# Moving three query loads and one pair of row copies to later steps in a fused attention and feed-forward kernel

## The chip, the cores and the metric

The kernel runs on one core of one Trainium2 chip, in one launch. The metric is the device time of that launch in microseconds (us); lower is better. Five engines work side by side, each through its own list of instructions in order: TensorE (PE in the profile; its weight loads are PEld), VectorE (DVE), ScalarE (ACT), GpSimd (POOL) and SyncE (SP). They meet at semaphores. POOL and SP also issue the transfers (DMAs) between the chip's main memory and its on-chip memory.

## The reference, cut to what matters

Inputs `q`, `k`, `v` have 4 batches, 8 heads, 768 positions and 64 numbers a head. Attention runs in chunks of 32 queries; each chunk sees 8 memory rows, 16 positions to the left and 8 to the right of itself. Its output is the input of a feed-forward block with a normalisation ahead of it and a residual.

```python
for c in range(nc):                       # chunks of 32
    q_c = q[:, :, c_start:c_end]
    k_full = concatenate([mem_k, k[:, :, l_start:r_end]])
    v_full = concatenate([mem_v, v[:, :, l_start:r_end]])
    scores = scale * matmul(q_c, k_full.T)
    a = softmax(scores)
    out[:, :, c_start:c_end] = matmul(a, v_full)
...
x = out.transpose(0, 2, 1, 3).reshape(B, S, H * D)          # 4 x 768 x 512
mu, var = mean(x), mean((x - mu) ** 2)
xn = (x - mu) / sqrt(var + 1e-06) * g_ln
return x + maximum(xn @ w_ch1, 0.0) @ w_ch2                 # 512 -> 2048 -> 512
```

## The kernel before

**Tiles and units.** The 4 x 768 tokens are 24 tiles of 128 (`t`), six to a batch; two tiles make a unit `u`, of 256 tokens, and there are 12 units. For a tile, `qk` makes scores on TensorE (`qk_products`, line 322), takes off the maximum on VectorE and exponentiates on ScalarE; `pt` transposes the weights P (line 353) and copies them on ScalarE (line 361); `val` multiplies them with V (line 373), normalises on VectorE (`tokens`) and subtracts the mean (`shift`, line 396, on POOL here); `root` squares on ScalarE (line 409) and makes the inverse root on POOL (lines 416 and 420); `turn_x` transposes the result (line 429) and copies it. A unit then goes up to 2048 in eight products (`up`, line 464) and down to 512 in seven (`down7`, line 643), the latter one unit behind.

**How the order is made.** Nothing is scheduled by a planner: the order on each engine is that in which the program is written. Up to unit 2 and from unit 8 on it is written out by hand. Units 3 to 7 are a loop over 16 steps: an even step ends with `up(u, step // 2)`, an odd one with `down7(u - 1, step // 2)`, and whatever `at(u, step, fn, ...)` put into the plan runs ahead of it, in the order in which it was put there.

**The loads of batches 2 and 3.** They are spread over the plan:

- `load_octets(i, half, src, b, lo, n)`, line 104, issues two DMAs on POOL (one for even, one for odd heads; each 48 partitions of 4 x 512 numbers, 192 KB in 16 bit, converted from 32 bit on the way) into `raw[i][half]`; `i` is 0 for k and 1 for q.
- `mix(i, half, engine)` copies `raw` into another order (line 261), k on VectorE at step 12 of the same unit and q on ScalarE at step 5 of the next. `later_k` and `later_q` transpose that on TensorE (line 274) and copy it into the key and query tiles.
- `load_v_head`, `load_v_ends`: V's rows, straight to their places, in runs of 128 bytes, also issued on POOL (lines 116, 121, 127, 131).
- `v_mem(b)`, line 155: two DMAs issued on SP (line 158), 120 KB each, which copy the memory rows from `memv16` (8 partitions) to two places of every group of V. `v_shared` (line 153), also on SP, copies rows of V that two groups share.

Batch 2's second half of k and q is loaded in unit 3, batch 3's halves in units 5 and 6. The first tile of batch 2, number 12, reaches `val` at step 4 of unit 5; the first of batch 3, number 18, right behind the loop.

**Stores.** SP also issues the stores of finished tiles (`store`, line 656, 256 KB), at the sixth and seventh part of `down7`, that is at steps 11 and 13.

**Waits that a program adds.** A DMA of POOL or SP waits for the DMA that last used its completion semaphore; POOL's take eight in turn, so each waits for the one eight DMAs back. Whatever stands behind a waiting instruction on its engine waits too.

Of the kernel before, what the change touches and what calls it, by code (L numbers as in the profile page):

```python
# [18 lines left out]
def kernel(  # L19
# [1078 lines left out]
    def at(u, step, fn, *args):  # L1098
        plan.setdefault((u, step), []).append((fn, args))
# [16 lines left out]
    for b in range(2, B):  # L1116
        u0 = 3 * b - 3
        for half in range(2):
            w = u0 - 1 + half
            if w > 2:  # L1120
                at(w, 1, load_octets, 0, half, k, b, 48 * half, 48)
                at(w, 3, load_octets, 1, half, q, b, 48 * half, 48)
                at(w, 12, mix, 0, half, "V")
            at(w + 1, 5, mix, 1, half, "A")
            for n, step in enumerate((1, 7 if w == 2 else 6, 11, 15)):
                if n < 2:
                    at(w + 1, step, later_k, b, half, n, "V")
                else:
                    at(w + 1, step, later_q, b, half, n - 2, "A")
            for n in range(8):  # L1130
                if w > 2:
                    step = (0, 2, 4, 12, 13, 14, 15, 16)[n]
                    at(w, step, load_v_head, b, 4 * half + n // 2, n % 2)
                else:
                    at(4, n // 2, load_v_head, b, n // 2, n % 2)
        at(u0 + 1, 0, load_v_ends, b)
        at(u0 + 1, 10 if b == 2 else 6, v_shared, b, 0, NG)
        if b == 2:
            at(3, 8, v_mem, b)
        else:  # L1140
            at(u0 + 1, 6, v_mem, b)
        at(u0, 14, mem_cols, KT[b % 2], memT[:, 4 * b : 4 * b + 4, :])
        at(u0, 14, mem_ends, KT[b % 2], memT[:, 4 * b : 4 * b + 4, :])
# [332 lines left out]
```

## Time and profile before

| What | Value |
|---|---|
| runs of the kernel, us | 224.4, 223.35, 224.49; median 224.4 |
| the profiled execution, us | 224.4 |
| its span, first to last instruction, us | 222.7 |
| mean granted TensorE clock | 0.997 |
| POOL's DMA queue (q0) | 38,416 packets, 14.48 MB, 56.3% of 16 engines' span |
| SP's DMA queue (q1) | 5,092 packets, 8.02 MB, 12.1% |
| queue of kind "instruction" (q8) | 28 packets, 0.46 MB, 0.8% |
| queue of kind "instruction" (q14) | 10 packets, 0.08 MB, 0.1% |

The profile describes one execution. Its span leaves out what lies ahead of the first and behind the last instruction, here 224.4 - 222.7 = 1.7 us. Times within it count from the span's start. Busy times are per engine and overlap; a share of the DMA queues is the time that their packets took against 16 engines working all the span. In the timeline, a bracket behind a row holds the idle time ahead of it on its engine and what ended it. The five units of the loop begin (first `up` product of each) at 70.28, 88.71, 105.71, 121.44 and 138.43 us; the loop's last product of the kind ends it at 155.40 us.

### The profile page before, as it was taken

The numbers are of one execution on the slowest core, as the hardware profiler recorded it, in microseconds if no ns is written. First come the engines' busy times: TensorE is split into PE (matmuls) and PEld (weight loads), VectorE is DVE, ScalarE is ACT, GpSimd is POOL, SyncE is SP. The second block draws the span as 40 slices with busy tenths as digits, with TensorE's granted clock in tenths as the row PEclk, the third lists the DMA queues.
The fourth block names the chain that finished last, engine by engine and source line by source line (L and its number), as shares of the span: only waits on it lengthen the run. The fifth ranks groups of instructions, "written<-read, shape, count | busy, mean of one in ns | idle before, by whom it ended". The sixth has DMA issues, their size and how long they took to land.

```text
span 222.7 us, 8335 instructions
## 1 busy us (share of the span) xinstructions
PE 212.9 (96%) x3581; PEld 187.3 (84%) x3581; DVE 175.9 (79%) x388; ACT 132.8 (60%) x262; POOL 134.2 (60%) x210
## 2 busy tenths in 40 slices
PE   6987999999999998999999999999999999999992
PEld 2555877789989988999989999999899899999981
DVE  1588767888898995994785996994889986888982
ACT  3198875886785397378347288288667734654000
POOL 7958399989999428947346937414377549830000
PEclk9999999999999999999999999999999999999998
DMA  5999999999998994993933993952000102001223
GB/s 74 193 205 204 213 212 207 136 168 149 119 99 106 185 97 71 141 84 86 180 43 88 133 112 71 103 95 84 25 3 3 39 11 81 17 4 49 94 97 96
DMA packets 43770, 23.24 MB, mean 104 GB/s; under 512 B 30068, under 2 KB 40372, under 8 KB 43684
## 3 DMA queue, kind: packets, MB, share of 16 engines
q0 software_dynamic: 38416, 14.48, 56.3%
q1 hardware_dynamic: 5092, 8.02, 12.1%
q8 instruction: 28, 0.46, 0.8%
q10 hardware_dynamic: 224, 0.20, 0.3%
q14 instruction: 10, 0.08, 0.1%
HBM read 29.02 MB, written 6.29 MB: 159 GB/s over the span
## 4 chain that ended last, share of the span: by engine, by line
PE 86%; DMA 9%; POOL 2%; issue 1%; DVE 0%; POOLq 0%
PE upb L464 22%; PE dnb L643 22%; DMA w1c<-in_moe_w_ch_dram 6%; PE one L464 5%; PE one L643 5%; PE dnb L464 4%; PE upb L643 4%; PE two L373 3%; DMA raw<-in_q_dram 3%; PE one L274 3%; PE dnb L578 2%; PE one L578 2%; PE one L322 2%; POOL raw L107 2%; PE one L353 2%; PE upb L490 2%
## 5 line engine op out<-in xcount | busy, mean ns | idle before, releaser
L464 PEld LDWEIGHTS <-w1c 128*128 128x128 f16 x640 | 67.3, 114 | 1.6 <-DMA w1c<-in_moe_w_ch_dram 0.4
L464 PE MATMUL upb<-xT,w1c 128*128 128x256 f16 x456 | 59.2, 274 | 0.0
L456 ACT ACTIVATE rT<-upb 128x512 f16<-128x512 f32 x55 | 32.1, 597 | 17.0 <-PE upb L464 16.7
L650 DVE SCALAR_TENSOR_TENSOR xs<-dnb,rstd,xs 128x256 f32<-128x256 f32 x55 | 26.3, 478 | 11.6 <-PE dnb L643 10.8
L643 PEld LDWEIGHTS <-RS 128*128 128x128 f16 x320 | 30.3, 98 | 3.2
L344 ACT ACTIVATE P<-sub 128x512 f16<-128x512 f32 x24 | 15.1, 632 | 22.3 <-DVE sub L334 22.3
L416 POOL TENSOR_SCALAR veps<-ssq 128x1 f32<-128x1 f32 x24 | 5.9, 248 | 35.0 <-ACT sq L409 34.1
L643 PEld LDWEIGHTS <-rT 128*128 128x128 f16 x240 | 22.9, 98 | 2.3
L643 PE MATMUL dnb<-T,RS 128*128 128x256 f16 x184 | 23.9, 273 | 0.0
L396 POOL TENSOR_SCALAR xn<-xs,nmean 128x512 f16<-128x512 f32 x17 | 12.6, 740 | 17.7 <-DVE nmean L389 13.5
L637 DVE TENSOR_TENSOR RS<-rT 128x1024 f16<-128x1024 f16 x18 | 13.5, 754 | 5.4 <-ACT rT L456 5.2
L409 ACT ACTIVATE sq<-xs,nmean 128x512 f16<-128x512 f32 x24 | 17.3, 721 | 0.2
L383 DVE CUSTOM_DVE_ANT_1 xs<-two,rec 128x512 f32<-128x512 f32 x24 | 16.6, 691 | 0.8
L643 PE MATMUL dnb<-w2c,rT 128*128 128x256 f16 x120 | 15.4, 273 | 0.0
L420 POOL TENSOR_TENSOR rstd<-veps,mhalf 128x1 f32<-128x1 f32 x24 | 13.8, 573 | 2.0
L116 POOL DMA_DIRECT2D V<-in_v_dram x16 | 13.5, 844 | 0.8 <-PE dnb L643 0.7
L241 DVE COPY KT<-one 128x192 f16<-128x192 f16 (+1 forms) x20 | 10.2, 548 | 3.3 <-PE one L228 2.5
L464 PE MATMUL one<-xT,w1c 128*128 128x256 f16 x96 | 12.5, 273 | 0.2 <-DMA w1c<-in_moe_w_ch_dram 0.2
L274 PEld LDWEIGHTS <-raw 96*128 96x128 f16 x192 | 10.4, 97 | 1.6 <-issue 1.1
L464 PE MATMUL dnb<-xT,w1c 128*128 128x256 f16 x88 | 11.3, 274 | 0.0
L361 ACT COPY PT<-one 128x512 f16<-128x512 f16 x14 | 8.2, 584 | 4.6 <-PE one L353 4.6
L373 PEld LDWEIGHTS <-PT 64*32 64x32 f16 x768 | 7.3, 93 | 4.2 <-issue 3.1
(197 smaller groups left out, 484.1 us busy)
## 6 DMA issues: line engine op xcount, KB each, us to landing
out_dram<-xs SPq DMA_DIRECT2D x21, 256.0 KB
raw<-in_k_dram POOLq DMA_DIRECT2D x16, 192.0 KB, 5.5
raw<-in_q_dram POOLq DMA_DIRECT2D x12, 192.0 KB, 5.5
w1c<-in_moe_w_ch_dram POOLq DMA_DIRECT2D x4, 512.0 KB, 11.8
w2c<-in_moe_w_ch_dram POOLq DMA_DIRECT2D x4, 512.0 KB, 14.0
V<-in_v_dram POOLq DMA_DIRECT2D x16, 77.0 KB, 3.8
raw<-in_v_dram POOLq DMA_DIRECT2D x4, 192.0 KB, 6.8
V<-V SPq DMA_DIRECT2D x2, 360.0 KB
```

The costliest lines, as they stand in the source:

```text
L116: nc.gpsimd.dma_start(out=V[b % 2][72:128, 0 : NG - 1, h, 0:64], in_=dram(v, base + 16 * D, [[64, 56], [64 * 64, NG - 1], [1, 64]]),)
L274: nc.tensor.matmul(out=pv[:, rows * r : rows * r + rows], lhsT=m[0:rows, jj, r, :], rhs=identity[0:rows, 0:rows], is_transpose=True, start ...
L344: nc.scalar.activation(out=P[t % 3], in_=sub[t % 2], func=ACTF.Exp, scale=0.125)
L373: nc.tensor.matmul(out=two[col : col + 32, 128 * h : 128 * h + 65], lhsT=PT[t % 3][rows, 2 * (h // 4) + h % 2, q0 : q0 + 32], rhs=V[b % 2] ...
L383: nc.vector.tensor_tensor_reduce(out=x.rearrange("p (h d) -> p h d", h=H), in0=free(two, 0, [[128, 8], [1, 64]]), in1=free(r, 0, [[1, 8], ...
L409: nc.scalar.activation(out=sq, in_=xs[t % 9], func=ACTF.Square, bias=nmean[t % 6], scale=1.0, accum_out=ssq[i],)
L420: nc.gpsimd.tensor_tensor(out=rstd[t % 9], in0=veps[i], in1=mhalf, op=ALU.pow)
L456: nc.scalar.activation(out=o, in_=i, func=ACTF.Relu)
L464: nc.tensor.matmul(out=p[:, 256 * hb : 256 * hb + 256], lhsT=free(w1c[hc // 4][:, dt, :], hc % 4, [[4, 128]]), rhs=xT[u % 3][:, dt, :], st ...
L637: nc.vector.tensor_tensor(out=R[k][:, lo:hi, :], in0=a[:, lo:hi, :], in1=b[:, lo:hi, :], op=op)
L643: nc.tensor.matmul(out=p[:, 0:256], lhsT=left[:, n, :], rhs=right(n), start=(n == 0 and not add), stop=(n == 7), skip_group_check=add,)
L650: nc.vector.scalar_tensor_tensor(out=x, in0=p[:, 0:256], scalar=rstd[t % 9], in1=x, op0=ALU.mult, op1=ALU.add,)
```

## The change

Two lines of the plan. Within units 3 and 5 the query load moves from step 3 to step 10, within unit 6 from step 3 to step 8. Batch 2's memory rows move from step 8 to step 12 of unit 3, which on SP is from ahead of unit 3's first store (step 11) to behind it.

```diff
             if w > 2:
                 at(w, 1, load_octets, 0, half, k, b, 48 * half, 48)
-                at(w, 3, load_octets, 1, half, q, b, 48 * half, 48)
+                at(w, 10 if w < 6 else 8, load_octets, 1, half, q, b, 48 * half, 48)
                 at(w, 12, mix, 0, half, "V")
...
         if b == 2:
-            at(3, 8, v_mem, b)
+            at(3, 12, v_mem, b)
         else:
             at(u0 + 1, 6, v_mem, b)
```

`w` is the unit in which a half of batch `b` is loaded. On TensorE, VectorE and ScalarE the order of instructions is the same as before. On POOL each of the three pairs of query DMAs now stands behind the shifts of both tiles of its unit, one V load and the first root, and ahead of the second root. No instruction is added or taken away.

## The prediction

> **What bounds the kernel now.** First the page's head: TensorE is busy nearly throughout, so only what leaves TensorE idle, or makes it do more, can set the end.
>
> ```profile
> span 222.7 us, 8335 instructions
> PE 212.9 (96%) x3581; PEld 187.3 (84%) x3581; DVE 175.9 (79%) x388; ACT 132.8 (60%) x262; POOL 134.2 (60%) x210
> ```
>
> Second, busy time by stretches, cut where the timeline shows the first up product of units 3, 4, 5, 6 and 7 (columns: stretch, length, then busy time and count of PE, PEld, DVE, ACT, POOL, granted clock, DMA share, GB/s).
>
> ```profile
> 70.28:88.71 18.43, 17.49 (x307) 16.16 (x306) 15.18 (x36) 11.26 (x21) 9.99 (x18) 1.00 0.92 117
> 88.71:105.71 17.00, 17.00 (x301) 15.81 (x298) 13.30 (x29) 11.17 (x21) 12.25 (x21) 1.00 0.97 103
> 105.71:121.44 15.73, 15.66 (x268) 14.39 (x266) 12.21 (x27) 8.53 (x17) 7.09 (x12) 1.00 0.62 97
> 121.44:138.43 16.99, 16.99 (x298) 15.67 (x297) 14.22 (x34) 10.69 (x20) 11.85 (x21) 1.00 0.94 112
> ```
>
> Only unit 3 has visible idle PE time: 18.43 - 17.49 = 0.94 us. Third, the chain of waits there: it stands inside one group of eight transposes (L274, line 274), after the seventh, and the releaser is "issue", so no data, semaphore or engine was waited for.
>
> ```profile
> 83.13 0.30 PE one L274 x7
> 83.43 0.94 issue
> 84.37 0.22 PE one L274
> ```
>
> A second, shorter hold stands in unit 5, in the middle of the score products (L322): 32 matmuls took 0.67 us there and 0.44 us in unit 6, 0.23 us more.
>
> ```profile
> 113.80 0.67 PE L322 MATMUL one<-KT,QD 64*32 64x64 f16 x32
> 130.21 0.44 PE L322 MATMUL one<-KT,QD 64*32 64x64 f16 x32
> ```
>
> What are the two? Count TensorE's instructions from where the first ends to where the second ends (84.36 to 114.09): 511 matmuls and 512 weight loads, 1,023. That is four times 256 but for one (a record can be missing). The DMA view has a queue of kind "instruction", q8: 28 packets of 16 KB in the run, 16,384 / 256 = 64 bytes an instruction. From 70.2 to 81.9 it moved nothing; its next packet lies in 81.9 to 83.0:
>
> ```profile
> q0 software_dynamic: 2485, 0.91, 89.4%
> q1 hardware_dynamic: 497, 0.77, 27.9%
> ...
> q0 software_dynamic: 240, 0.09, 66.5%
> q8 instruction: 1, 0.02, 5.6%
> ```
>
> (First two lines: 70.2 to 81.9; last two: 81.9 to 83.0.) Likewise none from 100.0 to 111.7, then one in 111.7 to 112.7. The packets begin at 81.97 and 111.72, last 0.98 and 0.94 us, and TensorE goes on 1.42 and 1.43 us after their ends. So I read both as TensorE out of instructions: block fetched late. Counted in TensorE instructions ahead of need, the fetch in quiet stretches starts 276 ahead (199.77 to 214.63) or 238 (98.89 to 109.34); these two started 38 and 110 ahead. At the normal lead the first would have started at about 75.9: it came 6 us late, while POOL's queue alone held 89% of 16 engines. [...]
>
> **The change, part by part.**
>
> *Nothing is added or removed.* TensorE, VectorE and ScalarE keep their instructions in the same order. On POOL three pairs of query loads (L107, 192 KB each) each move behind five instructions (two shifts, a V load, the two of a root); on SP two copies of the mem rows (L158, 120 KB each) move behind one store.
>
> *Taken out of the late fetch's way, unit 3.* Between 70.4 and 72.9 us the queues took: two stores, two k loads, two mem copies, a V load, two q loads. The loads of 1 KB packets landed slowly:
>
> ```profile
> L107 POOL DMA_DIRECT2D raw<-in_q_dram x2: 574/590/606, 72.3 to 72.9; - x2
> DMA to landing us min/median/max: 6.0/9.2/11.5
> ```
>
> Both q loads (384 packets of 1 KB, half of the 768 that ran until 83.8) and both mem copies (192 packets, 76.2 to 81.6) leave this stretch. By the q and k packets' pace in unit 5 (768 in 105.9 to 113.6, 100 per us) 384 fewer free 3.8 us, the mem copies some more; the fetch must start by 81.97 - 1.10 = 80.9, and 3.8 us earlier than 81.97 is 78.2. Gain between 0 (fetch still late) and the whole hold; I take the whole. Its size: unit 3 less unit 6, its twin in work, is 18.43 - 16.99 = 1.44 us; 0.44 of it is two extra transposes of P (L353, 0.22 us each on the chain); 1.00 us remains. Using unit 6 as the floor includes what ScalarE would take back: in unit 6 the transposes of x (L429, at 135.90) start 0.12 us late behind ScalarE's copy of PT, and unit 3 has that copy at 84.51 to 85.09, just where TensorE will then arrive (86.17 - 1.1 = 85.07).
>
> *Unit 5.* q leaves 106.3 to 107.5 us, half of the 1 KB packets; the fetch (started 111.72) was short by 0.23 us and 3.8 us are freed. Gain 0 to 0.23; I take 0.23.
>
> *Where they go, POOL.* Unit 3's pair lands behind the shift of step 8 (ends 83.69), ahead of the root:
>
> ```profile
> 83.01 0.68 POOL L396 TENSOR_SCALAR xn<-xs,nmean 128x512 f16<-128x512 f32 x1
> 84.70 0.19 POOL L416 TENSOR_SCALAR veps<-ssq 128x1 f32<-128x1 f32 x1 [1.01 <-ACT sq L409]
> ...
> 95.39 0.62 POOL L121 DMA_DIRECT2D V<-in_v_dram  x1
> 96.05 0.71 POOL L396 TENSOR_SCALAR xn<-xs,nmean 128x512 f16<-128x512 f32 x1
> ```
>
> Two issues at 0.59 us fill the 1.01 us of idle and push the root, fifteen V loads and the shift at 96.05 by 0.17 us. Who waits: the transposes L429 at 98.89, which arrive about 1.0 earlier, 97.9; the shift would end at 96.05 + 0.71 + 0.17 = 96.9. Cover 1.0 us, so 0. Were POOL made to wait (each load waits on the semaphore of the one eight back), the cover is smaller: the tightest had 1.1 us to spare (issued 86.17, landed 4.4 us later, reused at 91.70). Pushed by all of q's 3.8 us it would wait 2.7 and cost 1.7 us. I take 0, since the DMAs idle at 7% from 83.7 to 85.0 and can take q first, and POOL in unit 6 ran V loads right behind q without a wait. In units 5 and 6 the pairs fall ahead of ScalarE-bound roots, into 2.82 and 1.26 us of idle: 0.
>
> *Landings.* q is read by ScalarE's copies (L261) in the next unit: 96.66 in unit 4, so 95.6 then; issued at 83.7 and 84.3, with unit 5's worst 7.1 us, it lands by 91.4; with the worst row, 11.5, at 95.8, a cost of 0.2. Unit 7's copy runs at 146.38, q is issued near 134: 0. Mem rows: issued near 87 instead of 71.4, first read by L373 at 109.30: 0. SP's next store starts some 0.5 us later; nothing waits for it.
>
> *Next fetch.* In unit 4 one starts at 93.99 (195 instructions ahead), ends 95.05, and is needed at 97.84: spare 97.84 - 95.05 - 1.42 = 1.4 us. q should be through by 89, so 0; else see the second rival.
>
> Sum: 1.00 + 0.23 = 1.23 us. The profiled execution took 224.4 us (span 222.7 and 1.7 around it), equal to the median of the three runs. After unit 7 no idle on TensorE of this kind is seen, so the gain lasts: 224.4 - 1.2 = 223.2 us, 0.55% less.
>
> **The rivals.**
>
> *The load backlog is not what delays the fetch; nothing changes.* For it: one of the three runs took 223.35, 1.05 us less than the median, about one such hold, so the hold may come and go by itself. Against: the lag rises with 1 KB packets in flight at both places. Then 224.4 us. [...]
>
> *The late fetch moves to unit 4; slower.* There q, both mem copies, two stores and the V loads now meet in 84 to 95 us, where the DMA share is already 1.12 to 1.26. The fetch at 93.99 becomes late once it slips by over 1.4 us, and decides for slower once it slips by over 1.4 + 1.2 = 2.6. With unit 3's 6 us lag (it is 1.1 today) it slips 5, costs 3.6 and the time is 224.4 - 1.2 + 3.6 = 226.8. Against: no 1 KB packets are left then by my count, and under V loads alone lags were 1 to 2 us.
>
> *POOL's queue of V loads slips and x's transposes wait in unit 4.* 0.5 to 1.7 us as above: 223.7 to 224.9, say 224.2.
>
> *Only unit 3's hold goes half, or not unit 5's:* 223.6.
>
> **How the numbers follow.** Forecast 0.62, no effect 0.12, unit 4's fetch 0.08, POOL's slip 0.09, partial 0.09. A measurement of this kernel can tell about 0.5% (1.1 us) from no change, so the line lies at 223.3. The forecast, with ±0.4 us of its own, has some four fifths below it or better, and some of the rivals none: faster 0.58; slower 0.10 (unit 4's fetch and the end of POOL's slip); same 0.32. The range goes from 222.6 (forecast, and the small holds of 0.1 us gone as well) to 224.5, which takes in "no effect" and most of POOL's slip; the forecast's own range is 222.7 to 223.6.
>
> **What would show it.** Right: no "issue" on the chain in unit 3, its stretch at about 17.4 us; L322 in unit 5 at 0.44 us; an instruction packet before 80.9. Wrong: an "issue" of any size in unit 4, idle PE before L429 there released by xn, or the 0.94 us still in place while the q packets are gone.

## The result and the profile after

| | median, us | range, us | runs |
|---|---|---|---|
| before | 223.51 | 222.72 to 224.49 | 6 |
| after | 227.12 | 225.25 to 228.35 | 6 |

The changed kernel is slower: ratio 1.0157, 95% interval 1.0122 to 1.0193, where 0.55% less was forecast. Its profiled execution took 225.25 us, the shortest of its six runs; why the others take about 2 us more is taken up with the experiments, and stays open in part.

First the page's head of the changed kernel, and its busy time by stretches, cut again at the first up product of units 3, 4, 5, 6 and 7 (columns as in the prediction).

```profile
span 223.5 us, 8335 instructions
PE 213.2 (95%) x3581; PEld 187.4 (84%) x3581; DVE 175.2 (78%) x388; ACT 132.8 (59%) x262; POOL 134.2 (60%) x210
```

```profile
70.17:87.58 17.41, 17.41 (x307) 16.13 (x305) 15.13 (x36) 11.16 (x21) 9.72 (x17) 1.00 0.67 95
87.58:106.80 19.22, 17.18 (x301) 15.74 (x299) 13.49 (x29) 11.27 (x21) 13.95 (x23) 1.00 1.27 126
106.80:122.29 15.49, 15.49 (x268) 14.35 (x266) 12.21 (x27) 8.43 (x17) 6.56 (x12) 1.00 0.61 96
122.29:139.29 17.00, 17.00 (x298) 15.69 (x297) 14.25 (x34) 10.69 (x20) 11.84 (x20) 1.00 0.88 97
```

Unit 3 went from 18.43 to 17.41 us and unit 5 from 15.73 to 15.49: the 1.02 and 0.24 us that the prediction promised (1.00 and 0.23). But unit 4 went from 17.00 to 19.22. The sum, -1.02 - 0.24 + 2.22 = +0.96, is the difference of the two profiled executions (225.25 - 224.4 = 0.85) but for 0.1 us in the start-up.

TensorE's timeline in unit 4 shows the new hold, ahead of the transposes of x; first the kernel before, then the changed one:

```profile
98.89 0.39 PE L429 MATMUL one<-identity,xn 128*128 128x128 f16 x4
```

```profile
96.86 1.06 PE L464 MATMUL upb<-xT,w1c 128*128 128x256 f16 x8
99.97 0.40 PE L429 MATMUL one<-identity,xn 128*128 128x128 f16 x4 [2.04 <-POOL xn L396]
```

It waits for xn of tile 10, the shift on POOL. POOL's timeline there, again the kernel before (the row at L131) and then the changed one:

```profile
91.18 0.53 POOL L131 DMA_DIRECT2D V<-in_v_dram  x1
```

```profile
85.82 0.70 POOL L121 DMA_DIRECT2D V<-in_v_dram  x1
...
90.84 0.63 POOL L127 DMA_DIRECT2D V<-in_v_dram  x1
94.25 0.53 POOL L131 DMA_DIRECT2D V<-in_v_dram  x1 [2.77 <-DMA V<-in_v_dram]
...
99.22 0.70 POOL L396 TENSOR_SCALAR xn<-xs,nmean 128x512 f16<-128x512 f32 x1
```

POOL stands still for 2.77 us at L131: this load reuses the completion semaphore of the V load issued eight DMAs earlier, at 85.82, and that one has not landed. All that stands behind it on POOL, six V loads and the shift, moves back; the shift runs at 99.22 instead of 96.05. The landing of that V load (us from issue: least, median, most) before and after:

```profile
DMA to landing us min/median/max: 2.8/2.8/2.8
```

```profile
DMA to landing us min/median/max: 8.1/8.1/8.1
```

85.82 + 8.1 = 93.9, and POOL goes on at 94.25. What slowed it is seen in the DMA view of 90 to 92 us (queue; packets, MB, share of 16 engines), first the kernel before, then the changed one:

```profile
q0 software_dynamic: 1967, 0.22, 180.2%
q1 hardware_dynamic: 65, 0.11, 14.5%
```

```profile
q1 hardware_dynamic: 131, 0.20, 84.7%
q0 software_dynamic: 208, 0.02, 36.9%
```

POOL's queue (q0) moved 208 packets in place of 1,967, though eight V loads were waiting in it. SP's queue (q1) held the two mem-row copies (80 packets of 1,280 bytes) and a store (46 of 2,048), and its 131 packets took 0.847 x 16 x 2 / 131 = 0.21 us each. A store alone does not do this: in the kernel before, SP's packets in the same 2 us are a store's, and POOL's queue ran on beside them.

### The profile page after: what moved, and what is told of

Its sections match the earlier page's. It is cut to its first block, busy times and chain, and to the rows that moved or that the text cites. A ratio compares the mean times of both kernels' runs of the same rounds, so it can differ in the third digit from the quotient of the medians.

```text
span 223.5 us, 8335 instructions
## 1 busy us (share of the span) xinstructions
PE 213.2 (95%) x3581; PEld 187.4 (84%) x3581; DVE 175.2 (78%) x388; ACT 132.8 (59%) x262; POOL 134.2 (60%) x210
## 4 chain that ended last, share of the span: by engine, by line
PE 87%; POOL 5%; DMA 4%; DVE 1%; issue 1%; ACT 1%; POOLq 0%
PE upb L464 23%; PE dnb L643 22%; PE one L464 5%; PE one L643 5%; PE dnb L464 4%; PE upb L643 4%; DMA raw<-in_v_dram 4%; PE two L373 3%; PE one L274 3%; POOL raw L107 2%; PE dnb L578 2%; PE one L578 2%; PE one L322 2%; PE one L353 2%; PE upb L490 2%; PE one L429 2%
## 5 line engine op out<-in xcount | busy, mean ns | idle before, releaser
L420 POOL TENSOR_TENSOR rstd<-veps,mhalf 128x1 f32<-128x1 f32 x24 | 14.3, 597 | 2.0
L445 DVE TENSOR_TENSOR xT<-one,g_col 128x512 f16<-128x512 f16 x13 | 8.9, 685 | 3.2 <-PE one L429 3.0
L373 PEld LDWEIGHTS <-PT 64*32 64x32 f16 x768 | 7.4, 93 | 4.3 <-issue 3.1
L334 DVE TENSOR_TENSOR sub<-one,nmx 128x512 f32<-128x512 f32 x15 | 10.4, 691 | 0.6
```

Source lines behind the costliest of these rows:

```text
L373: nc.tensor.matmul(out=two[col : col + 32, 128 * h : 128 * h + 65], lhsT=PT[t % 3][rows, 2 * (h // 4) + h % 2, q0 : q0 + 32], rhs=V[b % 2] ...
L420: nc.gpsimd.tensor_tensor(out=rstd[t % 9], in0=veps[i], in1=mhalf, op=ALU.pow)
```

## The experiments

Theory A: the mem-row copies, meeting the V loads, hold them up; POOL then waits for a semaphore, and the shift behind it on POOL is late for TensorE. Theory B: the query loads, now ahead of the V loads in POOL's own queue, do it alone.

**The query loads alone**, and **the mem rows alone** (edits against the changed kernel).

```diff
-            at(3, 12, v_mem, b)
+            at(3, 8, v_mem, b)
```

> The three query loads stay at their later steps, the two mem-row copies go back to step 8 of unit 3. Theory A (the mem-row copies, issued near 86 us with the two stores, hold up the V loads, and POOL then waits 2.8 us at L131 for the V load eight back): POOL's wait at L131 goes, the V load issued near 85.8 lands within 6 us instead of 8.1, TensorE's wait for xn in unit 4 is under 0.3 us, the instruction stalls stay away, and the time is 222 to 223, against 223.5 before and 227.1 with the change. Theory B (the query loads ahead of the V loads alone do it): POOL waits 2 to 3 us as in the changed kernel, TensorE waits about 2 us for xn, 226 to 227.5.

```diff
-                at(w, 10 if w < 6 else 8, load_octets, 1, half, q, b, 48 * half, 48)
+                at(w, 3, load_octets, 1, half, q, b, 48 * half, 48)
```

> Only the mem-row copies move behind unit 3's first store; the query loads stay at step 3. Theory A: the copies meet the V loads at 88 to 93 us and slow them as in the changed kernel; with no query loads ahead of the V loads the first V load still lands early, so POOL waits for a later one or little: 223.5 to 225.5. Theory B: no wait of POOL, time 223 to 223.7 (the instruction stall in unit 3 shorter by what the copies no longer take).

Query loads alone: 223.34 us, ratio to before 0.9997 (0.9976 to 1.0018): the loss is gone, but the time is that of the kernel before and not the 222 to 223 expected. Between 84 and 105 us POOL waits for no landing and TensorE for no xn. The V load at 85.74 lands in 4.0 us, and the DMA view of 90 to 92 us of that run shows POOL's queue at full pace:

```profile
q0 software_dynamic: 2297, 0.26, 212.3%
```

Theory B falls. Mem rows alone: 224.14 us, ratio 1.0025 (1.0001 to 1.0049), inside the range of theory A. V loads land in 4.9 and 7.1 us, POOL's queue moves 859 packets in 90 to 92, and the waits of 84 to 105 us (who, for whom: us in total, times, longest) are

```profile
POOL V L116 <- DMA V<-in_v_dram: 1.9, 1, 1.9
...
PE one L429 <- POOL xn L396: 0.9, 1, 0.9
```

So the copies suffice to make the wait, and the query loads ahead, harmless alone, make it longer: 2.0 us on TensorE for both together.

**The mem rows later still**, behind the V loads.

```diff
-            at(3, 12, v_mem, b)
+            at(4, 10, v_mem, b)
```

> Query loads late as in the change; the mem-row copies later still, behind the copy of V's shared rows at step 10 of unit 4 (issued near 98 us, when the V loads have landed). Theory A: no POOL wait at L131, no TensorE wait for xn in unit 4, no instruction stall: 222 to 223, as with the query loads alone. Theory B: 226 to 227.5 as with the change.

223.54 us, ratio 1.0002 (0.9979 to 1.0025): the loss is gone, as theory A asks, but the time is that of before, not the 222 to 223 expected. Its profiled execution, the fastest of its twelve runs (222.69 us), has no hold left in units 3 to 7:

```profile
span 221.0 us, 8335 instructions
```

**The wait, taken off TensorE's way.** The change in full, with tile 10's shift on ScalarE.

```diff
-            at(u, step, val, t)
+            at(u, step, val, t, *(("A",) if t == 10 else ()))
```

> The whole change, but tile 10's shift in unit 4, which stands behind the V loads on POOL, is done by ScalarE. Both theories on what slows the V loads: POOL still waits about 2.8 us at L131, but if that wait costs time only through xn of tile 10, TensorE no longer waits for it and the time falls from 227.1 to 222.3 to 223.5. If something else in the change costs the time (its TensorE clock, the root behind the same queue, later loads), it stays at 225 to 227.

223.9 us, ratio 1.001 (0.9987 to 1.0033), a little above the range expected. POOL still waits, and no L429 row is left among the waits of 84 to 160 us; TensorE's one row there is of another kind:

```profile
POOL V L131 <- DMA V<-in_v_dram: 2.4, 1, 2.4
...
PE one L322 <- issue: 0.7, 1, 0.7
```

Of the change's 3.6 us, about 3.2 (227.12 - 223.9, medians of different rounds) go this way: through one shift behind one queue, with whatever follows such a wait. The row at L322 is a late instruction fetch in unit 5 (its packet ended at 112.96, TensorE went on at 114.42), although the query load is moved away from there in this kernel too. Eleven of the twelve runs took 222.93 to 224.88 us, one 227.41.

**The amount of copying.** Once more the same two copies, and one of the two only.

```diff
             at(3, 12, v_mem, b)
+            at(3, 12, v_mem, b)
```

> The changed kernel with the two mem-row copies of unit 3 issued a second time right behind the first (same data to the same places). Theory (the copies hold up the V loads): they run about 4.7 us longer beside the V loads, POOL's wait grows from 2.8 by 1 to 4 us, and the time from 227.1 to 228 to 231. Rival (the order on SP and the semaphores make the wait, not the copies' traffic): 227 as with the change.

```diff
-            at(3, 12, v_mem, b)
+            at(3, 8, v_mem, b, 0, NG, (32,))
+            at(3, 12, v_mem, b, 0, NG, (64,))
```

(`v_mem` takes the list of its places here.)

> The whole change, but only one of the two mem-row copies stands behind the store; the other is back at step 8. Theory (the copies' traffic holds up the V loads, by its amount): the V load issued near 85.7 lands between 4.0 us (no copy there) and 8.1 us (both) after issue, POOL's wait is 0 to 1.5 us in place of 2.8, TensorE's wait for xn in unit 4 under 1.2 us, and the time 223.3 to 224.8. Rival (one copy is enough, as any SP transfer there delays POOL): the wait stays over 2.3 us and the time is 226 to 227.5.

| copies beside the V loads | first V load's landing, us | POOL's waits for landings, us | TensorE's wait for xn, us | time, us | ratio to before, 95% |
|---|---|---|---|---|---|
| none (query loads alone) | 4.0 | 0 | 0 | 223.34 | 0.9976 to 1.0018 |
| one | 6.4 | 1.0 | 0.4 | 223.64 | 0.9996 to 1.0039 |
| two (the change, first profile) | 8.1 | 2.8 | 2.0 | 227.12 | 1.0122 to 1.0193 |
| four | 6.8 | 4.0, in four waits | 3.3 | 227.44 | 1.0091 to 1.0218 |

The waits in this table are from one profile each. They grow with the copying, which the rival of those two runs (any SP transfer there, whatever its size) does not explain: with one copy POOL waits 1.0 us where it asks for over 2.3. The time with four was under the 228 to 231 expected and cannot be told from that with two: the second pair ran behind the first (95 to 100 us, the first 88 to 93), and so spread the waits instead of lengthening the first. In the profile with four (227.9 us) the granted clock also fell to half, from 100.91 to 104.32; TensorE's wait for xn ended at 101.32.

**Unit 3's part alone.**

```diff
-                at(w, 10 if w < 6 else 8, load_octets, 1, half, q, b, 48 * half, 48)
+                at(w, 10 if w == 3 else 3, load_octets, 1, half, q, b, 48 * half, 48)
```

> Unit 3's part of the change alone: its query load at step 10 and the mem-row copies behind the store; the query loads of units 5 and 6 stay at step 3. Theory (all of the loss is made in units 3 and 4): 226.5 to 227.5, as the whole change. Rival (the loads moved in units 5 and 6 take part in it): 225 to 226 or less.

226.04 us in four runs, ratio 1.0115 (1.0069 to 1.016), between the ranges of the theory and of the rival. Its interval overlaps that of the whole change, and its profile (225.19 us) has the same hold, 2.1 us for xn. So most of the loss is made in units 3 and 4; whether units 5 and 6 add a part of it, four runs cannot tell.

**The kernel before, twice more.** Is the hold that the change was to remove there at all, usually?

> The kernel before once more, for a second profile. If the two late instruction fetches of the first profile (1.10 and 0.25 us) are usual, they show again, at 84 and 114 us. If they come and go (the first profile's 224.4 lies above the median of 223.5), one or both are shorter or gone, and the span is about 221.5 instead of 222.7.

> The same as the run before this one, a third profile of the kernel before: holds of 1.10 and 0.25 us at 84 and 114 us if they are usual, shorter or gone if they come and go with the run.

Not in these two. Spans of 221.3 us both times (223.02 and 223.06 us), no wait of TensorE in units 3 to 7, and unit 3 is as short as in the changed kernel (the first of the two):

```profile
70.20:87.61 17.41, 17.41 (x306) 16.13 (x305) 15.02 (x36) 11.15 (x21) 9.45 (x16) 1.00 0.97 123
```

The fetch for the same block ended at 81.47 and 79.16 in these two. In the first profile it ended at 82.95 and made a hold of 1.10 us, so it would be late from 81.85 on, 0.4 and 2.7 us after these two ends. The hold is real but a matter of the run.

**The changed kernel again**, for the runs near 227 us.

> The changed kernel once more, for a second profile: its first one shows the fastest of its runs (225.25, median 227.1). Theory (POOL's wait for the V load eight back delays xn of tile 10): a time near 227 shows a longer wait of POOL and a TensorE wait for xn of about 4 us in place of 2.0. Rival (TensorE's clock falls after the wait, granted clock 0.98 to 0.99 in the slower runs): the wait stays at 2 us and matmuls behind it take longer, at a lower granted clock.

> The changed kernel again, timed beside the others. Theory (a wait of TensorE of 2 us costs 2 us, and one of some 3 us or one that meets a stretch of low clock costs 3.4 us at half the clock on top, 1.7 us): times in two groups, near 225 with a mean granted clock of 0.995 to 1.0, and near 227 with one lower by about 0.0075 (half of 3.4 us in 226). Rival: one group, with no tie between time and clock.

> The changed kernel once more, for a profile of its common time near 227. If it takes that: after the wait for xn in unit 4 the granted clock is 0.5 for some 3.4 us and the 128 x 256 matmuls there are 214 ns apart in place of 109. If it takes near 225: no such stretch.

The first gave 224.87 us and the first profile over again (POOL waits 2.7, TensorE 2.0), so it told nothing on the runs near 227. The last gave 226.27 with a wait for xn of 2.6 us and no stretch of low clock. The five timed runs lay at 226.56 to 227.42 (median 227.0, ratio 1.0155, 1.0126 to 1.0183): one group, not two, and one of them (226.56) with a mean granted clock of 1.0, so the two groups that I expected are not there. The profile of the run at 227.42 shows two things more. TensorE's timeline:

```profile
96.52 0.54 PE L322 MATMUL one<-KT,QD 64*32 64x64 f16 x31
99.04 0.20 PE L322 MATMUL one<-KT,QD 64*32 64x64 f16 x1 [1.98 <-issue]
99.17 1.06 PE L464 MATMUL upb<-xT,w1c 128*128 128x256 f16 x8
100.41 0.44 PE L429 MATMUL one<-identity,xn 128*128 128x128 f16 x4 [0.18 <-POOL xn L396]
100.65 1.91 PE L643 MATMUL dnb<-T,RS 128*128 128x256 f16 x8
```

Here TensorE first waits 1.98 us for instructions (the fetch of the block that unit 4 needs began at 96.5, in the other three profiles of the changed kernel at 93.8 to 94.2), then only 0.18 for xn: the two waits lie over each other, and either alone would have held it. Then eight matmuls take 1.91 us in place of 1.04. The stretches of that run (PEclk is the third figure from the end):

```profile
96.00:100.64 4.64, 2.48 (x80) 1.84 (x78) 3.28 (x8) 2.88 (x5) 4.39 (x8) 1.00 1.47 97
100.64:104.05 3.41, 3.41 (x20) 2.44 (x17) 1.23 (x3) 1.11 (x2) 1.24 (x2) 0.50 0.68 118
```

After the hold the clock is granted at half for 3.41 us; half the work of that time is lost, 1.7 us. So a run of the changed kernel pays 2.0 to 2.6 us in waits, and this one 1.7 us more. How often the clock falls stays open: the mean clock of a run does not tell, since a run of the query loads alone with 0.988 took 223.08 us, and in the third profile of the kernel before (0.989, 223.06 us) the fall lies in the start-up, from 18.41 to 21.82. This is also the only profile of a run at the usual 227; that the others near 227 owe their 2 us to the same is not shown.

No version tried here is shown to beat the kernel before.

## Why the prediction was wrong

**What held.** The reading of both holds as late instruction fetches. The runs also bear out that the loads delay them: the packet for unit 3 began at 75.8 to 77.5 us in all ten profiles with that unit's query load moved, and at 78.0 to 82.0 in the three of the kernel before. That both holds were gone by the amounts forecast is partly luck: two further profiles of the kernel before do not have them either, and unit 5's came back once with the query loads late (0.73 us, with the shift on ScalarE). (The block of 256 was read from a count; the page fits it: 3,581 matmuls and 3,581 weight loads in 28 packets of q8 are 255.8 each, if all are TensorE's. From 84 to 114 us there are five crossings of a block; two of them were late.) POOL's own order cost what was said, as the run with the query loads alone shows: its shift runs at 96.26 (forecast 96.2), no wait.

**The base.** I took the profiled execution's 224.4, the median of three runs, as typical. It held 1.26 us of holds that two further profiles do not have. The rival "the hold may come and go by itself" was thus the truer one on the gain: the two kernels whose profiles have none of these holds and no wait for xn (the query loads alone, the mem rows later still) take the time of the kernel before, as far as twelve runs of each can tell.

**The step that failed** is the one on POOL's queue: "Were POOL made to wait (each load waits on the semaphore of the one eight back), the cover is smaller", priced at up to 1.7 us and then taken at 0, "since the DMAs idle at 7% from 83.7 to 85.0 and can take q first, and POOL in unit 6 ran V loads right behind q without a wait". Both reasons were about the query loads, and for them they were right: alone they cost POOL nothing. What I costed at nothing without asking was the other edit: "Mem rows: issued near 87 instead of 71.4, first read by L373 at 109.30: 0". I priced the copies by when their own data is needed, not by what their 192 packets do to the V loads that POOL was issuing at that time. The second rival names this meeting, but asks only what it does to the instruction fetch. The runs showed in its place a wait of POOL of 2.8 us that the copies make and the query loads alone do not, and behind it 2.04 us of TensorE ahead of L429, released by xn, which the prediction had named as a sign of being wrong. The rows were in the trace of the kernel before: those packets ran from 76.2 to 81.6 us, and a V load issued at 71.63 beside them and the query loads landed only at 82.4.

**The sizes.** The rival "POOL's queue of V loads slips" had 0.5 to 1.7 us and 0.09; measured were 2.0 to 2.6 us on TensorE. The cover of 1.0 us was about right. That POOL's wait of 2.8 us is close to the 2.7 of the upper bound is luck: the 2.7 was worked out from the 3.8 us of the query packets, which alone made no wait. xn came 3.2 us late, more than POOL's wait, as the V loads ahead had started 0.35 us later. The rival "the late fetch moves to unit 4" came about once in four profiles of the changed kernel, with 1.98 us where it had 3.6. Neither had the clock's fall in its price. So the range ended at 224.5, below all six runs.

## What to carry to other kernels

A transfer that is moved must be priced by what it meets in its new place, each queue's landings there included (here a V load's went from 2.8 to 8.1 us), and not only by when its data is needed. A hold seen in one profile may not be the kernel's usual state: compare it with the spread of the runs, or take a second profile, before counting its removal as gain. A compute instruction behind many loads on POOL can take over their waits for a semaphore: here 2.77 us at L131, and the shift ran at 99.22 in place of 96.05. A step of the critical path is better put on another engine (the shift on ScalarE took away about 3.2 of the 3.6 us).

## What the runs showed of the hardware

- POOL's queue of 128-byte packets nearly stopped beside the mem-row copies (packets of 1,280 bytes) and a store: 208 packets in the 2 us from 90 to 92. It moved 859 with the copies but no query loads ahead of the V loads, 1,967 beside a store alone (the kernel before), and 2,297 in the run where SP's queue had nothing in those 2 us. Which part of the path they compete for was not tried. The copies read from and write to 8 partitions each; whether that matters is open too.
- Four times TensorE stood still within a group with no data, semaphore or engine waited for; the profile has 0.94 us of "issue" (unit 3 of the kernel before), 0.19 (unit 5 there, on its weight loads), 0.7 (the shift on ScalarE) and 1.98 (the run at 227.42). That each is an instruction block fetched late is my reading: TensorE went on 1.42 and 1.43 (the kernel before), 1.46 (the shift on ScalarE) and 1.61 us (the run at 227.42) after the end of a packet of q8.
- The granted clock fell to 0.50 for one stretch of 3.41 us after a stretch of the same length in which TensorE was busy for 1.42 us (97.22 to 100.64 in the run at 227.42). With four copies it fell after one busy for 0.52 us (97.50 to 100.91), in the third profile of the kernel before in the start-up after one busy for 1.78 us (14.99 to 18.41). In the changed kernel's first profile it stayed at 1.00 after 3.40 us busy for 1.35 us (96.60 to 100.00), and in the run at 226.27 after 3.41 us busy for 0.77 us (97.60 to 101.01). So TensorE's busy time in the 3.4 us ahead does not tell by itself whether the clock falls; what does was not shown.
